# Scale rows and weight units issued earlier, and the slot work of the second-last expert one step sooner, in a one-core retention and expert kernel

## The chip, the cores and the metric

One core of one Trainium2 chip runs the whole kernel. The metric is the device time of one launch in microseconds. The kernel before took 427.85 us (median of three runs, 426.66 to 427.98). All times inside the kernel are counted from the start of the span of one profiled execution.

Engines: TensorE (PE, with its weight loads PEld), VectorE (DVE), ScalarE (ACT), GpSimd (POOL) and SyncE (SP). SP does no arithmetic here: it issues nearly all transfers between DRAM and the on-chip memory, in the order of the program, and where one of them has to wait, all behind it wait too. POOL issues the transfers that pick rows by an index list (gather) or scatter them.

## The reference, cut to what matters

```python
# 1 retention: q, k, v are (4, 8, 768, 64)
for t in range(768):
    state = gamma * state + outer(k[t], v[t]);  y[t] = scale * q[t] @ state
x = y as (3072 tokens, 512)
# 2 each token goes to one of 8 experts
e = argmax(x @ w_gate)
scale = softmax(x @ w_gate)[e] * sigmoid(x @ w_output_gate)[e]
x[token] = scale * (relu(x[token] @ w1[e]) @ w2[e])      # w1 512x1024, w2 1024x512
# 3 soft slots: 32 slots, 4 for each of 8 second experts
logits = x @ phi
slot_input = softmax(logits, over tokens).T @ x
slot_out   = relu(slot_input @ w1b[e]) @ w2b[e]
out = softmax(logits, over slots) @ slot_out
```

## The kernel before, in words

The kernel has three stages. The retention stage walks over 24 tiles of 128 tokens and writes the rows `x` to a DRAM table `xs`. Each row of `xs` has 512 values and behind them the token's scale (tile `sv`), which is written by a transfer of its own, `scale_put`. The last three tiles' scales are computed after the loop over the tiles (`gate_scale`), from line 694 on. There too a table `wps` of partial products is written in two halves of 512 KB, the second (L726) waiting for ACT's last copies into `fsum`.

Then the tokens of one expert at a time are gathered from `xs` (tile `xg`, L755, 3 or 4 gathers of up to 128 rows for each expert), scaled (L902 or L904), transposed (`x_mm`, L911) and multiplied. The first gather needs the index list `xidx` (L746) and every row of `xs`. All engines pass a branch (L868) there, whose body is for experts that are over their capacity.

The expert stage takes the 8 experts in turn, and each expert in 8 steps `f` (the count `g` runs over all 64 steps). In step `g` PE makes a block of the hidden layer (`l1`, L933, 12 products), ACT rectifies it (L938), and the weight block for step `g + 2` is split in two parts, `wh` by ACT (L222) and `wl` by DVE (L223), from a tile `r` that SP has loaded (`load_w`, L214). The products go into one of two buffers in turn, so step `g` needs the rectified block of step `g - 2` to be out. The second layer isn't formed: its product with `phi` is (`wq_mm`, tile `wps`, L243), from units `wt` of 512 KB (`wq_load`, L234), three for each expert, in a pool of three. For the first expert the three units wait until all its gathers have landed; the units of the second expert are issued behind steps 3 and 4, behind the loads of two or more `r` tiles and of a part of the table (`wpp`, L949).

Beside the steps of an expert the slot work of the expert before it is done (`behind`): sums of logits (`lps` L963, `lsum` L984), the exponentials, the product of the hidden blocks with them (`slot_h`, tile `gps`, L1046), copies of that to `gr` (`slot_s`, L1053), their sum (`slot_t`, tile `gsum`, L1059), the product with the second weights `w` (`slot_in`, tile `slo`, L1068; loaded by L954), and the sum into `acc` (`slot_acc`, L1072). For the second-last expert `slot_in` and `slot_acc` come behind the last step of the last expert, among the first operations of the last expert's own slot work, which nothing overlaps.

Each engine runs its instructions in the order in which the program is written; pools of tiles decide when a load may start. In the last expert's steps SP also starts to load the weights `m` of the last stage (`load_m2`, L269, 128 tiles of 256 KB in all) into tiles that come free. The last stage multiplies the slots by these weights (`fh` L1246, `so` L1283), and 24 output transfers of 256 KB each end the kernel.

Of the kernel before, what the change touches and what calls it, by code (L numbers as in the profile page):

```python
# [22 lines left out]
E = 8  # L23
# [4 lines left out]
KD = DM // 128  # L28
KF = FF // 128
# [9 lines left out]
IO, UMM, QA = 6, 2, 1  # L39
# [98 lines left out]
def retention_moe_kernel(ctx, tc, qt, kt, kn, vn, gates, moe_w1, moe_w2,  # L138
                         moe2_phi, moe2_w1, moe2_w2, consts, out, dbg=None):
    nc = tc.nc  # L140
    _, off, ni, na, nb = _consts()
# [60 lines left out]
    def after(inst, earlier):  # L202
        for other in earlier:
            tc.add_manual_dep(inst.ins, other.ins.name,
                              mybir.DependencyInfo(mybir.DependencyClass.Sync, mybir.DependencyReason.DATA),
                              reason="order of transfers")
# [9 lines left out]
    def split_w(g):  # L216
        if g >= G:
            return
        t = raw_t.pop(g)
        hi = whl.tile([128, DM], F32R, tag="wh1", name="wh1")  # L220
        lo = whl.tile([128, DM], F32R, tag="wl1", name="wl1")
        nc.scalar.activation(out=hi, in_=t, func=ACTF.Copy)  # L222
        nc.vector.tensor_tensor(out=lo, in0=t, in1=hi, op=ALU.subtract)  # L223
        w1_t[g] = (hi, lo)
# [7 lines left out]
    def wq_load(k, q, n, pool, tag):  # L232
        t = pool.tile([128, n * FF], F32, tag=tag, name="wt")
        get = nc.sync.dma_start(out=t, in_=moe_w2[1, bass.ds(er[k], 1), :, q * FF:(q + n) * FF].rearrange("o p d -> (o p) d"))  # L234
        for h in range(n):
            wtt[k, q + h] = [t[:, h * FF + g * 256:h * FF + g * 256 + 256] for g in range(4)]
        return get
# [8 lines left out]
    def wq_add(k):  # L246
        nc.vector.tensor_tensor(out=parts[k], in0=wacc.pop(k), in1=parts[k], op=ALU.add)
# [28 lines left out]
    def load_m2(pool, tag, w=1):  # L276
        w = min(w, NM2 - len(m2_t))
        if w > 0:
            m2_into(pool.tile([128, w * 512], F32, tag=tag, name="m2"), w, (pool, tag, w) if w < 3 else None)
# [37 lines left out]
    with ExitStack() as pa:  # L317
# [96 lines left out]
        def first_copy(e):  # L414
            nc.scalar.copy(out=fsum[:, e, :], in_=facc.pop(e))
# [170 lines left out]
        def gate_scale(i):  # L586
            if i not in ENDS:
                return
            t, n = ENDS[i]
            sm = gs.pop(t)  # L590
            one_ = lambda k: sm[:, k, 0, 0:n]
            nc.vector.tensor_reduce(out=one_(8), in_=sm[:, 6, 0:n, :], axis=AX.X, op=ALU.add)
            nc.vector.tensor_scalar(out=one_(9), in0=one_(7), scalar1=1.0, scalar2=None, op0=ALU.add)
            nc.vector.scalar_tensor_tensor(out=one_(10), in0=one_(8), scalar=1e-9, in1=one_(9), op0=ALU.add, op1=ALU.mult)
            scl[t] = sc2.tile([128, 3, DX - DM], F32, tag="sv", name="sv")
            nc.vector.reciprocal(out=scl[t][:, 0:n, :], in_=bc(one_(10), n, DX - DM))
# [39 lines left out]
        def scale_put(i):  # L636

            if i not in ENDS:
                return
            t, n = ENDS[i]  # L640
            nc.sync.dma_start(out=xs[t * 128:(t + n) * 128, DM:DX].rearrange("(u p) o -> p u o", p=128), in_=scl.pop(t)[:, 0:n, :])
# [81 lines left out]
            first_mm(e)  # L723
        for e in range(4, E):
            first_copy(e)
        nc.sync.dma_start(out=wps[:, 4:E], in_=fsum[:, 4:E])  # L726
        gate_scale(i)
        scale_put(i)
        load_er(0)
        load_w(0)  # L730
        load_w(1)
# [158 lines left out]
    with ExitStack() as pb:  # L890
# [60 lines left out]
        def load_w2(e, fs, pool=w2p, tag="w2"):  # L951
            for f in fs:
                w2n[e, f] = pool.tile([128, DM], F32, tag=tag, name="w2")
                nc.sync.dma_start(out=w2n[e, f], in_=moe_w2[0, bass.ds(er[e], 1), :, f * DM:(f + 1) * DM].rearrange("o p d -> (o p) d"))  # L954
# [109 lines left out]
        def slot_in(e):  # L1064
            ps = slo[e] = ps_1.tile([128, DM], F32, tag="C", name="slo")
            for f in range(KF):
                i = f % 4
                nc.tensor.matmul(out=ps[32 * i:32 * i + 32, :], lhsT=gts[e][:, f, :], rhs=w2n.pop((e, f)),  # L1068
                                 start=(f < 4), stop=(f >= 4), skip_group_check=True)

        def slot_acc(e):
            nc.vector.scalar_tensor_tensor(out=acc, in0=acc, scalar=sms.pop(e)[:, 4:5], in1=slo.pop(e), op0=ALU.mult, op1=ALU.add)  # L1072

        def behind(e, f):

            if not 0 <= e < E:
                return
            if f == 0:
                logits(e, 1)
                if e:  # L1080
                    slot_in(e - 1)
                h_tr(e, 6)
                h_tr(e, 7)
            elif f == 1:
                logit_sum(e)
            elif f == 2:
                p_exp(e)
            elif f == 3:
                p_tr(e)
            elif f == 4:  # L1090
                slot_h(e)
                c_tr(e)
            elif f == 5:
                slot_s(e)
                c_exp(e)
            elif f == 6:
                slot_t(e)
                c_put(e)
            if 2 < f < 7:
                load_w2(e, (2 * f - 6, 2 * f - 5))  # L1100

        load_er(1)

        after(wq_load(0, QA, 1, wup, "wu"), gets[0])
        for q in range(QA + 1, KD):
            wq_load(0, q, 1, wup, "wu")
        part_load(0)
# [8 lines left out]
        for g in range(G):  # L1116
            e, f = divmod(g, KF)
            if f == 0:
                load_er(e + 2)
            if e + 1 < E and f < len(XT[e + 1]):  # L1120

                gather(e + 1, (f,))
                if f:
                    after(gets[e + 1][f], [relu[-1]])
            split_w(g + 2)
            if e and f == 1:

                if e > 1:
                    slot_acc(e - 2)
                logit_parts(e - 1)  # L1130
            if g < G - 3:
                load_w(g + 3)
            else:
                load_m2(wraw, "r1")
            if g > 3 and g % 2 and len(m2_t) < NPRE:
                load_m2(m2p, "m2", 2)
            if f in (4, 5) and e + 1 < E:
                for j in range(2 * f - 8, min(2 * f - 6, len(XT[e + 1]))):
                    x_scale(e + 1, j)
            if f == KF - 1 and e + 1 < E:  # L1140

                xps = x_mm(e + 1, "ABDr", sorted(((j, kk) for kk in range(KD) for j in range(len(XT[e + 1]))),
                                                 key=lambda b: XT[e + 1][b[0]] < 128))
                l1(g, lambda: [x_split(e + 1, ps) for ps in xps])
            else:
                l1(g)
            behind(e - 1, f)


            if g == UMM:  # L1150
                wq_mm(0, ps_1, "C")
                wq_add(0)
            if f == (1 if e else UMM):
                wq_turn(e, sp.tile([128, KF, NS], F32, tag="wp", name="wp"))
            if e + 1 < E:
                if f == (2 if e else 3):
                    part_load(e + 1)
                if e == 0 and f in (3, 4):
                    for q in ((1, 2), (3,))[f - 3]:
                        wq_load(1, q, 1, wup, "wu")  # L1160
                if f == (3 if e else 6):

                    wq_mm(e + 1, ps_1, "A" if e else "C")
                    wq_add(e + 1)
            if g == KF - 1:
                wq_load(2, 1, 1, wup, "wu")
                wq_load(2, 2, 1, wup, "wu")
            if g == KF:
                wq_load(2, 3, 1, wup, "wu")
            if e and e + 2 < E and 4 <= f < 7:  # L1170
                wq_load(e + 2, f - 3, 1, wup, "wu")
            elif G - 13 < g < G - 9:
                load_m2(wup, "wu", 2)
            if g == G - 6:
                load_w2(e, range(4), xp, "xy")
            if g >= G - 2:

                for i, tag in enumerate(("wh1", "wl1")):
                    load_w2(e, (2 * f - 8 + i,), whl, tag)
            if f == 4:  # L1180
                logits(e, 0)
            if f == 5:

                mask(e)
            if f >= 5:
                h_tr(e, 2 * f - 10)
                h_tr(e, 2 * f - 9)
        e = E - 1
        logits(e, 1)
        logit_parts(e)  # L1190
        slot_in(e - 1)
        slot_acc(e - 1)
        logit_sum(e)
        load_m2(whl, "wh1")
        load_m2(whl, "wl1")
        for _ in range(KD):
            load_m2(xtp, "xh")
            load_m2(xtp, "xl")
        for _ in range(8):
            load_m2(w2p, "w2")  # L1200
        h_tr(e, 6)
        h_tr(e, 7)
        for _ in range(NH):
# [20 lines left out]
        c_exp(e)  # L1224
        c_put(e)
        for _ in range(4):
            load_m2(xp, "xy")
        for _ in range(2):
            load_m2(whl, "wh1")
            load_m2(whl, "wl1")  # L1230
# [162 lines left out]
```

## Time and profile before

| | |
|---|---|
| median of 3 runs | 427.85 us (426.66 to 427.98) |
| profiled execution | 427.91 us |
| its span, first to last instruction | 426.1 us |
| outside the span | 1.8 us |
| PE / DVE / ACT / POOL busy | 379.5 / 260.9 / 165.6 / 108.0 us |
| moved by DMA | 132.96 MB, 312 GB/s over the span |
| chain that ended last | PE 73%, DVE 9%, DMA 7%, ACT 4% |

The terms of the chain say what was late at each moment. An average over the span says little: PE is busy for 89% of it, but the places where it waits are few and each has its own cause, and behind the expert stage the DMA engines are full while PE isn't.

### The profile page before, as it was taken

The numbers are of one execution on the slowest core, as the hardware profiler recorded it, in microseconds if no ns is written. First come the engines' busy times: TensorE is split into PE (matmuls) and PEld (weight loads), VectorE is DVE, ScalarE is ACT, GpSimd is POOL, SyncE is SP. The second block draws the span as 40 slices with busy tenths as digits, with TensorE's granted clock in tenths as the row PEclk, the third lists the DMA queues.
The fourth block names the chain that finished last, engine by engine and source line by source line (L and its number), as shares of the span: only waits on it lengthen the run. The fifth ranks groups of instructions, "written<-read, shape, count | busy, mean of one in ns | idle before, by whom it ended". The sixth has DMA issues, their size and how long they took to land.

```text
span 426.1 us, 11539 instructions
## 1 busy us (share of the span) xinstructions
PE 379.5 (89%) x4407; PEld 284.7 (67%) x4407; DVE 260.9 (61%) x681; ACT 165.6 (39%) x368; POOL 108.0 (25%) x116
## 2 busy tenths in 40 slices
PE   2989999998639999999999999999999996799990
PEld 2877777786428777777877877787679872225560
DVE  1698989988723276575675664864757655414250
ACT  1532322223324365454545545543555421112232
POOL 2203333321033113043252431620612122020020
PEclk9999999999958999999999999999999999699996
DMA  7999999999958798977969969969778789999998
GB/s 270 403 420 334 307 314 338 304 280 327 251 161 316 222 368 287 385 279 237 403 225 329 376 203 357 358 192 386 248 223 338 238 263 318 388 398 407 392 346 289
DMA packets 68002, 132.96 MB, mean 312 GB/s; under 512 B 10628, under 2 KB 30082, under 8 KB 65634
## 3 DMA queue, kind: packets, MB, share of 16 engines
q1 hardware_dynamic: 61154, 120.17, 80.2%
q0 software_dynamic: 3344, 8.34, 6.5%
q10 hardware_dynamic: 3440, 3.63, 2.6%
q8 instruction: 36, 0.59, 0.6%
q14 instruction: 28, 0.23, 0.2%
HBM read 117.89 MB, written 14.25 MB: 310 GB/s over the span
## 4 chain that ended last, share of the span: by engine, by line
PE 73%; DVE 9%; DMA 7%; ACT 4%; issue 3%; SPq 1%; ACTq 1%; another core or an unknown queue 0%; POOL 0%; POOLq 0%; DVEq 0%
PE hps L933 30%; PE s L447 5%; PE o L480 5%; PE gps L1046 5%; PE fh L1246 4%; PE slo L1068 4%; PE so L1283 3%; PE lps L963 3%; PE wps L243 3%; PE o L471 2%; DMA r<-in_moe_w_dram 2%; DMA raw<-in_qt_dram 2%; PE xps L911 2%; PE st L494 2%; PE g L545 2%
## 5 line engine op out<-in xcount | busy, mean ns | idle before, releaser
L933 PE MATMUL hps<-xh,wh 128*128 128x416 f32 (+2 forms) x256 | 92.9, 363 | 0.1
L933 PE MATMUL hps<-xl,wh 128*128 128x416 f32 (+2 forms) x256 | 90.1, 352 | 0.3 <-DVE xl L921 0.2
L933 PE MATMUL hps<-xh,wl 128*128 128x416 f32 (+2 forms) x256 | 89.5, 350 | 0.0
L223 DVE TENSOR_TENSOR wl<-r,wh 128x512 fp32r<-128x512 f32 x64 | 43.4, 680 | 57.9 <-ACT wh L222 47.3
L938 ACT ACTIVATE h<-hps 128x416 f32<-128x416 f32 (+2 forms) x64 | 32.6, 510 | 68.7 <-PE hps L933 67.1
L222 ACT ACTIVATE wh<-r 128x512 fp32r<-128x512 f32 x64 | 40.2, 630 | 48.9 <-DMA r<-in_moe_w_dram 38.2
L933 PEld LDWEIGHTS hps<-xh,wh 128*128 128x128 f32 x256 | 48.7, 190 | 15.5 <-issue 13.4
L1029 POOL DMA_INDIRECT ctok<-ce,xidx x29 | 30.1, 1040 | 100.9 <-DVE ce L1026 94.5
L933 PEld LDWEIGHTS hps<-xl,wh 128*128 128x128 f32 x256 | 48.8, 190 | 2.2 <-DVE xl L921 1.2
L933 PEld LDWEIGHTS hps<-xh,wl 128*128 128x128 f32 x256 | 48.7, 190 | 0.6
L755 POOL DMA_INDIRECT xg<-xs,xidx x29 | 30.4, 1047 | 70.3 <-ACT h L938 49.5
L457 DVE TENSOR_TENSOR sS<-s,csa 128x512 f32<-128x512 f32 x48 | 30.4, 674 | 14.4 <-PE s L447 14.4
L447 PE MATMUL s<-raw 64*128 64x128 f32 x384 | 31.9, 301 | 8.0 <-DMA raw<-in_qt_dram 7.7
L945 DVE STREAM_TRANSPOSE hB<-h 128x416 f32<-128x416 f32 (+2 forms) x64 | 34.4, 576 | 0.0
L447 PEld LDWEIGHTS s<-raw 64*128 64x128 f32 x384 | 26.7, 201 | 10.7 <-DMA raw<-in_qt_dram 5.5
L480 PE MATMUL o<-sS,raw 128*64 128x128 f32 x384 | 27.1, 285 | 0.0
L512 ACT COPY xT<-o 128x512 f32<-128x512 f32 x24 | 13.9, 580 | 32.0 <-PE o L480 32.0
L429 POOL TENSOR_TENSOR k<-raw,cs 128x512 f32<-128x512 f32 x20 | 21.9, 1110 | 16.4 <-DMA raw<-in_qt_dram 11.1
L911 PE MATMUL xps<-cs,xg 128*128 128x128 f32 (+2 forms) x116 | 15.7, 285 | 9.2 <-ACT wh L222 7.9
L480 PEld LDWEIGHTS o<-sS,raw 128*64 128x64 f32 x384 | 21.2, 140 | 3.7 <-issue 3.4
L1046 PE MATMUL gps<-hB,pd 32*32 32x256 f32 x816 | 19.8, 394 | 3.6 <-DVE pd L1000 3.6
L911 PEld LDWEIGHTS xps<-cs,xg 128*128 128x128 f32 (+2 forms) x116 | 12.8, 148 | 13.6 <-issue 11.7
(178 smaller groups left out, 532.6 us busy)
## 6 DMA issues: line engine op xcount, KB each, us to landing
m<-in_moe_w_dram SPq DMA_DIRECT2D x41, 512.0 KB
wt<-in_moe_w_dram SPq DMA_DIRECT2D x32, 512.0 KB
r<-in_moe_w_dram SPq DMA_DIRECT2D x64, 256.0 KB
w<-in_moe_w_dram SPq DMA_DIRECT2D x64, 256.0 KB
m<-in_moe_w_dram SPq DMA_DIRECT2D x36, 256.0 KB
xs<-xr SPq DMA_DIRECT2D x32, 192.0 KB
raw<-in_kt_dram SPq DMA_DIRECT2D x5, 1024.0 KB
raw<-in_kn_dram SPq DMA_DIRECT2D x5, 1024.0 KB
```

Of the source, the lines that this page charges most:

```text
L222: nc.scalar.activation(out=hi, in_=t, func=ACTF.Copy)
L223: nc.vector.tensor_tensor(out=lo, in0=t, in1=hi, op=ALU.subtract)
L447: nc.tensor.matmul(out=ps[h][:, p, :], lhsT=kq(i, p, 0)[r], rhs=kq(i, p, 1)[r], start=True, stop=True, tile_position=(64 * h, 0), skip_gro ...
L457: nc.vector.tensor_tensor(out=sS[i][:, h], in0=sps.pop((i, h)), in1=con("dm", 128)[:, 4 * h:4 * h + 4, :], op=ALU.mult)
L480: nc.tensor.matmul(out=o_at(i, p, h), lhsT=vals(i, 2 * p + h), rhs=s[:, h, p, :], start=(i % NCH == 0 and n < 4), stop=True, skip_group_ch ...
L755: gets.setdefault(e, []).append(nc.gpsimd.indirect_dma_start(out=t[0:r, :], out_offset=None, in_=xs[:, :], in_offset=bass.IndirectOffsetOn ...
L911: nc.tensor.transpose(out=ps[kk][:, j * 128:j * 128 + r], in_=xg[e][j][0:r, kk * 128:(kk + 1) * 128], identity=ident[0:r, 0:r])
L933: nc.tensor.matmul(out=ps, lhsT=a[:, kk * 128:(kk + 1) * 128], rhs=x[e][kk][:, 0:c], start=(n == 0), stop=(n == 11))
L938: relu.append(nc.scalar.activation(out=hs[g][:, 0:c], in_=ps, func=ACTF.Relu))
L945: nc.vector.transpose(out=hB[e][:, 0:NB[e], f, :], in_=hs[e * KF + f][:, 0:c].rearrange("p (b t) -> p b t", t=32))
L1029: put = nc.gpsimd.indirect_dma_start(out=ctok[:, :], out_offset=bass.IndirectOffsetOnAxis(ap=xidx[0:r, e, j:j + 1], axis=0), in_=cn[0:r, j ...
L1046: nc.tensor.matmul(out=ps[a][32 * j:32 * j + 32, :], lhsT=pd[q, b, :], rhs=hB[e][q, b].rearrange("p f t -> p (f t)"), start=(i == 0), stop ...
```

## The change

Five places change. (1) After the loop over tiles, the last scales are put (`scale_put`) ahead of the second half of `wps` on SP. (2) The first unit of the first expert waits for its first two gathers and not for all three. (3) The units of the second expert are issued right behind the products with the first expert's units (`g == UMM`), ahead of what SP issued there before. (4) For the second-last expert, `slot_s` moves from step 5 to 4, `slot_t` from 6 to 5, `slot_in` into step 6 and `slot_acc` into step 7. Its second weights are loaded in steps 1 to 4 and not 3 to 6. (5) In the last expert's first two steps, four `m` tiles are loaded into the buffers of gathered rows, where the last expert's first four weight tiles went; these go to the pool `w2p`, behind `slot_in`, followed by four `m` tiles.

```diff
         for e in range(4, E):
             first_copy(e)
+        gate_scale(i)
+
+        scale_put(i)
         nc.sync.dma_start(out=wps[:, 4:E], in_=fsum[:, 4:E])
-        gate_scale(i)
-        scale_put(i)
         load_er(0)
...
-        def behind(e, f):
+        def behind_one(e, f):
...
-            if 2 < f < 7:
+
+        def behind(e, f):
+            behind_one(e, f)
+            if e >= 0 and 2 < f < 7:
                 load_w2(e, (2 * f - 6, 2 * f - 5))
 
+        def behind_last(e, f):
+
+            if f < 4:
+                behind_one(e, f)
+            elif f == 4:
+                slot_h(e)
+                c_tr(e)
+                slot_s(e)
+            elif f == 5:
+                slot_t(e)
+                c_exp(e)
+            elif f == 6:
+                slot_in(e)
+                c_put(e)
+            elif f == 7:
+                slot_acc(e)
+            if 0 < f < 5:
+                load_w2(e, (2 * f - 2, 2 * f - 1))
+            elif f == 6:
+                load_w2(e + 1, range(4))
+                for _ in range(4):
+                    load_m2(w2p, "w2")
+
         load_er(1)
 
-        after(wq_load(0, QA, 1, wup, "wu"), gets[0])
+        after(wq_load(0, QA, 1, wup, "wu"), gets[0][:2])
...
             split_w(g + 2)
+            if G - KF <= g < G - KF + 2:
+                load_m2(xp, "xy")
+                load_m2(xp, "xy")
...
-            behind(e - 1, f)
+            (behind if e < E - 1 else behind_last)(e - 1, f)
...
             if g == UMM:
                 wq_mm(0, ps_1, "C")
                 wq_add(0)
+                for q in range(QA, KD):
+                    wq_load(1, q, 1, wup, "wu")
...
-                if e == 0 and f in (3, 4):
-                    for q in ((1, 2), (3,))[f - 3]:
-                        wq_load(1, q, 1, wup, "wu")
...
-            if g == G - 6:
-                load_w2(e, range(4), xp, "xy")
...
-        slot_in(e - 1)
-        slot_acc(e - 1)
...
-        for _ in range(8):
-            load_m2(w2p, "w2")
...
         for _ in range(4):
-            load_m2(xp, "xy")
+            load_m2(w2p, "w2")
```

SP's order behind the loop over tiles: `xs<-xr` are the rows of the last tiles, `xs<-sv` their scales, `wps<-fsum` the halves of the table.

```order
 L721 DMA wps<-fsum 128x1024
-L726 DMA wps<-fsum 128x1024
 L641 DMA xs<-sv 128x3x16
+L729 DMA wps<-fsum 128x1024
 L198 TENSOR_LOAD ordi
```

The scales now stand between the two halves of the table.

SP's order in the first expert's steps before, from the load of step 6's weights (`r`) on; `ISA` rows set registers:

```order
L214 ISA
L214 DMA r_3706<-in_moe_w_dram 128x512
L949 ISA
L949 DMA wpp<-wps 128x256
L234 ISA
L234 DMA wt<-in_moe_w_dram 128x1024
L234 ISA
L234 DMA wt<-in_moe_w_dram 128x1024
L214 ISA
L214 DMA r_3733<-in_moe_w_dram 128x512
L234 ISA
L234 DMA wt<-in_moe_w_dram 128x1024
```

And in the changed kernel, the same six transfers:

```order
L234 ISA
L234 DMA wt<-in_moe_w_dram 128x1024
L234 ISA
L234 DMA wt<-in_moe_w_dram 128x1024
L234 ISA
L234 DMA wt<-in_moe_w_dram 128x1024
L214 ISA
L214 DMA r_3712<-in_moe_w_dram 128x512
L950 ISA
L950 DMA wpp<-wps 128x256
L214 ISA
L214 DMA r_3735<-in_moe_w_dram 128x512
```

The three units have gone ahead of the weights of steps 6 and 7 and of the part of the table.

PE's order behind the last expert's last step before (`hps` is the hidden block, `slo` the second-last expert's product with the second weights):

```order
L933 MATMUL hps<-xh,wl_6594 128x384
L963 MATMUL lps<-h,wp 32x384 x4
L1068 MATMUL slo<-w_6503,gt 32x512
L1068 MATMUL slo<-w_6505,gt 32x512
L1068 MATMUL slo<-w_6584,gt 32x512
L1068 MATMUL slo<-w_6586,gt 32x512
L1068 MATMUL slo<-w_6624,gt 32x512
L1068 MATMUL slo<-w_6626,gt 32x512
L1068 MATMUL slo<-w_6670,gt 32x512
L1068 MATMUL slo<-w_6672,gt 32x512
L984 MATMUL lsum<-ls,same_r 128x384
L984 MATMUL lsum<-ll,same_r 128x384
```

And the same place in the changed kernel:

```order
L934 MATMUL hps<-xh,wl_6607 128x384
L964 MATMUL lps<-h,wp 32x384 x4
L985 MATMUL lsum<-ls,same_r 128x384
L985 MATMUL lsum<-ll,same_r 128x384
L1047 MATMUL gps<-hB,pd 32x256 x48
```

The eight products have left the place between `lps` and `lsum`; they stand one hidden block earlier.

## Rows read from the trace of the kernel before

**Rows 1.** The waits behind line 755, 113 to 117.4 us: duration min/median/max

```profile
L755 POOLq EVENT_SEMAPHORE  x4: 43/43/2550, 113.4 to 114.3; - x4
```

**Rows 2.** SP's issues in order of time, 110 to 132 us: start, us, engine, line

```profile
112.94 0.36 SPq L726 DMA_DIRECT2D wps<-fsum  x1
113.39 0.39 SPq L641 DMA_DIRECT2D xs<-sv  x1
...
125.83 1.42 SPq L234 DMA_DIRECT2D wt<-in_moe_w_dram  x3
```

**Rows 3.** DVE in order of time, 112 to 126 us; in brackets the idle time before

```profile
112.45 0.45 DVE L596 RECIPROCAL sv<-sm 128x48 f32<-128x48 f32 x1
...
115.25 0.19 DVE L746 TENSOR_REDUCE xidx<-lx 128x4 int32<-128x32 f32 x1
...
125.64 0.48 DVE L902 TENSOR_SCALAR xg<-xg 128x512 f32<-128x512 f32 x1 [2.02 <-DMA xg<-xs,xidx]
```

**Rows 4.** Chain that ended last, 104 to 165 us: start, us, what

```profile
120.60 5.02 DMA xg<-xs,xidx
...
127.37 8.80 PE hps L933 x36
...
144.32 5.31 DMA wt<-in_moe_w_dram
```

**Rows 5.** ACT in order of time, 122 to 151 us

```profile
123.06 0.72 ACT L904 ACTIVATE xg<-xg 128x512 f32<-128x512 f32 x1 [0.16 <-DMA xg<-xs,xidx]
...
134.47 0.63 ACT L222 ACTIVATE wh<-r 128x512 fp32r<-128x512 f32 x1 [2.09 <-DMA r<-in_moe_w_dram]
...
140.85 1.32 ACT L904 ACTIVATE xg<-xg 128x512 f32<-128x512 f32 x2
142.08 0.48 ACT L938 ACTIVATE h<-hps 128x384 f32<-128x384 f32 x1
147.94 0.63 ACT L222 ACTIVATE wh<-r 128x512 fp32r<-128x512 f32 x1 [5.38 <-DMA r<-in_moe_w_dram]
```

**Rows 6.** PE in order of time, 106 to 170 us

```profile
136.10 1.50 PE L243 MATMUL wps<-wt,phi 128*32 128x256 f32 x24
...
144.92 0.33 PE L933 MATMUL hps<-xh,wh 128*128 128x384 f32 x1
...
149.68 0.64 PE L243 MATMUL wps<-wt,phi 128*32 128x256 f32 x8 [1.52 <-DMA wt<-in_moe_w_dram]
```

**Rows 7.** Stretches: length, busy us of PE, PEld, DVE, ACT, POOL; clock, DMA share, GB/s

```profile
118.30:131.80 13.50, 7.58 (x25) 6.27 (x26) 4.82 (x9) 4.02 (x8) 3.71 (x4) 0.50 0.66 204
...
344.00:350.00 6.00, 6.00 (x45) 4.71 (x42) 2.31 (x7) 1.73 (x5) 0.00 (x0) 1.00 0.79 267
350.00:357.00 7.00, 5.79 (x38) 3.21 (x37) 4.77 (x12) 0.98 (x2) 2.98 (x3) 1.00 0.86 280
370.00:410.00 40.00, 38.95 (x449) 18.27 (x449) 12.76 (x48) 9.34 (x22) 4.45 (x5) 0.96 1.04 395
```

**Rows 8.** PE in order of time, 352 to 370 us

```profile
353.04 0.49 PE L963 MATMUL lps<-h,wp 128*32 128x384 f32 x1
353.23 2.02 PE L1068 MATMUL slo<-w,gt 128*32 128x512 f32 x13
...
355.46 0.33 PE L984 MATMUL lsum<-ll,same_r 128*128 128x384 f32 x1
```

**Rows 9.** DVE in order of time, 326 to 372 us

```profile
354.09 0.56 DVE L971 TENSOR_TENSOR ll<-lps,ls 128x384 fp32r<-128x384 f32 x1 [0.99 <-issue]
355.78 0.75 DVE L1072 SCALAR_TENSOR_TENSOR acc<-acc,smb,slo 128x512 f32<-128x512 f32 x1 [1.14 <-PE lsum L984]
356.45 0.55 DVE L986 TENSOR_TENSOR msk<-lsum,msk 128x384 f32<-128x384 f32 x1
```

**Rows 10.** Chain that ended last, 165 to 350 us: the product `slo` inside a step

```profile
331.37 1.72 PE slo L1068 x16
```

**Rows 11.** SP's issues in order of time, 338 to 358 us

```profile
342.63 5.71 SPq L954 DMA_DIRECT2D w<-in_moe_w_dram  x4
```

More of the change, by code (lines that the diff above doesn't have):

```diff
@@ L725, in retention_moe_kernel @@
             first_copy(e)
-        nc.sync.dma_start(out=wps[:, 4:E], in_=fsum[:, 4:E])
         gate_scale(i)
         scale_put(i)
+        nc.sync.dma_start(out=wps[:, 4:E], in_=fsum[:, 4:E])
         load_er(0)
```

## The prediction

> **What bounds the kernel now.** I read the stretches first, then PE in order of time for the places where it waits, then the chain, and last the engine or queue that each wait names. PE is the bound inside the expert stage: in 344 to 350 us it is busy for all of the 6.00 us [rows 7]. Behind it the transfers are full: from 370 to 410 us the DMA share is 1.04 at 395 GB/s [rows 7]. So a microsecond is won where PE waits, or where bytes of the last stage move earlier. The change touches three such places.
>
> The first is the pause between retention and experts. POOL's first gather stands in a wait that begins at 114.3 and takes 2.55 us, to 116.85 [rows 1]. The list `xidx` is there from 115.25 + 0.19 = 115.44 [rows 3]. What is left to wait for are the writes into `xs`, of which the scales are the last: issued at 113.39, behind the second half of `wps` at 112.94 [rows 2]. The third gather takes 5.02 us [rows 4], DVE scales its tile at 125.64 [rows 3], and the first expert product starts at 127.37 [rows 4].
>
> The second is a wait of PE of 1.52 us at 149.68 for a unit of the second expert [rows 6], which the chain shows as 5.31 us of transfer from 144.32 [rows 4]. The third is the passage behind the last step: `lps` ends at 353.53, and DVE reaches `msk` at 356.45 [rows 8, 9].
>
> **Part 1, the scales and the first units.** The scales are ready at 112.45 + 0.45 = 112.90 [rows 3] and can now be issued some 0.45 us earlier, and their bytes no longer follow 512 KB. At 395 GB/s those are 1.33 us, together 1.78; but the list isn't there before 115.44, so at most 116.85 - 115.44 = 1.41 us can be won, and nothing at least. The first half of `wps` and the rows are still ahead of them, so I take 0.9, two thirds of the upper end. `wps` is later by the scales' own issue of 0.39 us [rows 2]; it is read only after 125.83 [rows 2], which hides that.
>
> Releasing the first unit after two gathers lets three units, 1.5 MB, start beside the third. The second gather's tile is worked on from 123.06 [rows 5], so at 122.2 in the changed kernel; the third would end at 125.64 - 0.9 = 124.7 without them. Between lie 2.5 us in which they meet. The cost is between zero and 2.5 (its rest takes twice as long); the nearest row is the third gather itself, 5.02 us with nothing beside it for most of its time, so it isn't short of bandwidth, and I take 0.2. That leaves 0.7. PE's clock is 0.50 from 118.3 to 131.8 [rows 7], the 1.2 GHz level, after PE had stood idle; 4.4 us of the first expert's products run in it. If the rise follows the work, all 0.7 arrive; if it stays where it is, half. I take **0.6 us won**.
>
> The Trainium skill speaks against this edit. On the page "DMA: Bandwidth & Descriptors", in the section on queues, rings and completion order, it says that each DMA engine takes turns between the queues that have work for it, a packet at a time. The gathers and the units are on different queues, so by that rule the third gather would get every second turn. No row here has both at once.
>
> **Part 2, the units of the second expert.** The wait of 1.52 us goes. In its place: the three units start as their tiles come free, from a third of the 1.50 us product on, 136.10 + 0.50 = 136.6 [rows 6]. Behind them in SP's order, and behind their 1.5 MB, is now the `r` of step 6. ACT splits that tile (0.63), scales two gathered tiles (1.32) and only then rectifies step 4 (0.48), as it did at 140.85 to 142.56 [rows 5]; step 6 takes that buffer and started at 144.92 [rows 6]. The nearest row for an `r` behind three units: issue of the first unit at 125.83 [rows 2], split of the `r` at 134.47 on its landing [rows 5], 8.6 us. By bytes alone, 1.8 MB at 395 GB/s, it is 4.6. With 8.6 step 6 could start at 136.6 + 8.6 + 2.43 = 147.6, 2.7 us late, a net loss of 1.2; with 4.6 nothing is late, a net gain of 1.5. The row had a part of the table and a POOL gather between, so I take 7.0: 146.0, 1.1 us late, **0.4 us won**. ACT's other wait there, 5.38 us for the next `r` at 147.94 [rows 5], loses its cause too, as that `r` no longer stands behind the units; left alone, it would have held the scaled tiles until 147.94 + 0.63 + 1.32 = 149.9, so the unit wait alone was never worth its full 1.52.
>
> **Part 3, the slot work of the second-last expert.** No instruction is added. The product `slo` costs 1.72 us inside a step [rows 10]; in front of `lsum` it took until 353.23 + 2.02 = 355.25 [rows 8]. There it covered the making of `ls` and `ll`, which ends at 354.65 [rows 9]. PE has no idle time in the step that takes it, so `lps` ends 1.72 later, at 355.25. From there 354.65 - 353.53 = 1.12 to `ll`, 0.33 of `lsum`, 0.10 to `msk`: 356.80, against 356.45. `acc`, which stood ahead of `msk` on DVE from 355.78 [rows 9], is out of the way; that is in this sum. So **0.35 us lost**. The ends: 1.37 won if the step hides all of `slo`, 1.72 lost if nothing comes back. `slot_s` and `slot_t` only change steps; ACT's two copies now stand ahead of a weight split, which has a step and a half in hand.
>
> **Part 4, SP's queue at the end.** In step 6 SP meets four weight tiles that may not start before `slo` has read theirs, at about 350. The loads of before at 342.63 to 348.34 and behind them [rows 11] have to wait behind that. From 344 to 350 the kernel before moved 6 x 267 = 1.6 MB [rows 7]; the changed one moves little. Four tiles, 1.05 MB, have gone earlier instead, leaving 0.55 MB. From 350 to 357 the share was 0.86 at 280 GB/s [rows 7]; with a full queue at 395, 0.8 MB more go there. I take **0**, between 0.6 won and 2.7 lost (the 1.05 MB at 395 GB/s, if nothing is made up).
>
> **Sum.** 0.6 + 0.4 - 0.35 = 0.65 us won: 427.91 - 0.65 = 427.26 for the profiled execution. That execution is 0.06 above the median of the runs, so 427.2.
>
> **Rivals.** A: faster. The `r` of step 6 comes in time, and part 1 wins 0.9: 0.9 + 1.5 - 0.35 = 2.05, 425.8. If PE, busy earlier, also leaves the lower clock earlier, up to half of the 4.4 us come on top, 423.6. For it: the DMA engines are not full there, and the split tiles are needed late. Against: the 8.6 us of the row.
>
> B: slower. The hole in SP's queue isn't made up, and the last stage, at a share of 1.04 for 40 us [rows 7], ends later by the 2.7 us: 429.9. It decides from a lag of 1.9 us on (the 0.65 and 1.28). For it: the share, and that everything on SP stands behind one wait. Against: before, 350 to 357 wasn't full, and nothing in the last stage waits for a transfer on PE.
>
> C: change (1) doesn't do what it says, because the gather waits for another transfer or the landing isn't earlier. Then 0.6 are missing: 427.8.
>
> D: the third gather shares its engines with the units and takes all of the 2.5 us longer: 427.2 + 2.3 = 429.5. That is what the turns of the Trainium skill's page would make of it.
>
> **How the numbers follow.** The forecast has 0.46, A 0.33, B 0.10, C 0.06, D 0.05. About 0.3%, 1.28 us, is what a measurement of this kernel can tell from no change: below 426.6 is faster, above 429.1 slower. Faster: A and 0.04 of the forecast's lower edge, 0.37. Slower: B and D, 0.15. Within: 0.48. The forecast's own range is 426.4 to 428.4; the range reaches to A without an early clock and to most of B, 425.0 to 429.3.
>
> **What would show it.** Right: POOL's first wait ends near 116; PE has no wait ahead of its unit products in the first expert, but one of about a microsecond ahead of step 6, with ACT late; `msk` starts 0.3 us later from the end of step 7 of the last expert; SP issues nothing for some 7 us ahead of the second-last expert's `slo`, and the DMA share of the 7 us behind is near 1. Wrong: step 6 not late (A); the third gather's landing not earlier (C, D); output transfers that end later by more than the expert stage does (B).

## The result, and the profile after

| | before | after |
|---|---|---|
| median of 19 runs each | 427.51 us (424.19 to 432.11) | 432.2 us (427.54 to 436.2) |
| ratio | | 1.0089, 95% interval 1.0065 to 1.0113 |
| profiled execution | 427.91 us | 429.17 us |
| its span | 426.1 us | 427.4 us |
| clock over the span | 0.963 | 0.958 |

The change costs 0.89%, 3.8 us. The ratio leaves out the slow runs, among them two of the 19 of the changed kernel, and so is smaller than the quotient of the two medians. The forecast was 427.2 with a range up to 429.3; by the ratio the time is 431.3, outside the range, on the slower side. The profiled execution is one of the shorter ones of the changed kernel and shows only 1.3 us of the loss; the rest is read from the experiments. I take the four parts in turn.

**Part 1: the pause between retention and experts.** POOL in order of time, then SP's issues (start, us, engine, line; the idle time before in brackets), in the changed kernel:

```profile
116.07 1.27 POOL L756 DMA_INDIRECT xg<-xs,xidx  x1 [10.27 <-DVE lim L767]
117.64 1.04 POOL L756 DMA_INDIRECT xg<-xs,xidx  x1 [0.30 <-issue]
118.98 1.01 POOL L756 DMA_INDIRECT xg<-xs,xidx  x1 [0.31 <-issue]
```

```profile
112.61 0.38 SPq L641 DMA_DIRECT2D xs<-sv  x1
113.08 0.44 SPq L729 DMA_DIRECT2D wps<-fsum  x1
...
122.91 1.64 SPq L234 DMA_DIRECT2D wt<-in_moe_w_dram  x3
```

The first gather starts at 116.07, as soon as DVE's short operations behind the list end; and the third at 118.98, where it was 120.60 [rows 4]. The product with the first expert's units starts at 133.75 instead of 136.10 [rows 6], 2.35 us earlier. The first unit is issued only at 122.91, and the third gather's tile is scaled at 123.97, so the two met for some 1.1 us and not for the 2.5 that the prediction reckoned with.

**Part 2: steps 4 to 6 of the first expert.** SP, ACT, PE and the chain in order of time (the chain: start, us, what), and three stretches (length, busy us of PE, PEld, DVE, ACT, POOL, then clock, DMA share, GB/s):

```profile
134.45 1.52 SPq L234 DMA_DIRECT2D wt<-in_moe_w_dram  x3
136.60 0.33 SPq L214 DMA_DIRECT2D r<-in_moe_w_dram  x1
```

```profile
137.60 0.49 ACT L939 ACTIVATE h<-hps 128x384 f32<-128x384 f32 x1 [2.73 <-PE hps L934]
143.45 0.63 ACT L222 ACTIVATE wh<-r 128x512 fp32r<-128x512 f32 x1 [5.37 <-DMA r<-in_moe_w_dram]
143.99 1.32 ACT L905 ACTIVATE xg<-xg 128x512 f32<-128x512 f32 x2
145.21 0.47 ACT L939 ACTIVATE h<-hps 128x384 f32<-128x384 f32 x1
```

```profile
133.75 1.50 PE L243 MATMUL wps<-wt,phi 128*32 128x256 f32 x24
...
145.73 0.53 PE L934 MATMUL hps<-xh,wh 128*128 128x384 f32 x1 [3.00 <-ACT h L939]
146.06 0.52 PE L934 MATMUL hps<-xl,wh 128*128 128x384 f32 x1
...
149.57 1.50 PE L243 MATMUL wps<-wt,phi 128*32 128x256 f32 x24
```

```profile
136.60 6.77 DMA r<-in_moe_w_dram
...
145.73 3.91 PE hps L934 x12
```

```profile
134.40:143.40 9.00, 8.34 (x60) 6.62 (x52) 1.44 (x3) 0.96 (x2) 2.55 (x2) 1.00 0.95 299
143.00:145.70 2.70, 0.00 (x0) 0.00 (x0) 0.69 (x1) 2.25 (x5) 0.00 (x0) 1.00 0.86 333
145.70:149.50 3.80, 3.77 (x12) 3.54 (x12) 2.33 (x4) 2.62 (x5) 0.00 (x0) 0.55 0.67 205
```

The weights `r` of step 6 are issued behind the three units and land 6.77 us later. ACT stands in their split for 5.37 us (0.63 us of work), scales two gathered tiles, and only at 145.21 rectifies step 4. PE, which takes that buffer in step 6, waits 3.00 us. Then there is a second price: after the wait the granted clock is 0.55, the 1.2 GHz level for most of the stretch; the products follow each other at 0.32 us, and the twelve of step 6 take 3.91 us. Twelve take 2.31 at 2.4 GHz (tail, below), so 1.6 us more are lost. The wait of 1.52 us for a unit [rows 6] is gone: the unit product at 149.57 has none. Net, by the end of that product: 3.0 + 1.6 - 1.52 = 3.1 us lost where the forecast had 0.4 won.

A part of it comes back. Before, PE then waited for DVE ahead of the second expert's `lsum`, and from its last product of one hidden block (160.03) to the first of the next (161.53) it took 1.50 us; the changed kernel has no wait there and takes 0.55 (160.79 to 161.34). The first two rows are of before, the third of the changed kernel; L243 is here the third expert's unit product:

```profile
161.24 0.45 PE L984 MATMUL lsum<-ll,same_r 128*128 128x384 f32 x1 [0.37 <-DVE ll L971]
...
166.48 1.50 PE L243 MATMUL wps<-wt,phi 128*32 128x256 f32 x24
```

```profile
166.29 1.50 PE L243 MATMUL wps<-wt,phi 128*32 128x256 f32 x24
```

From the first expert's unit product to the third's it takes 30.38 us before and 32.54 in the changed kernel: 2.2 us lost. With part 1's gain the changed kernel is 0.19 us ahead at the third product, so in this pair of executions the front loses nothing, and what its span is longer, 1.3 us, is lost behind it. Over all traces that distance is 32.5 to 35.3 us in the five kernels with three units ahead of step 6's weights, and 29.4 to 32.1 in the nine others; the means, 33.7 and 30.8, lie 2.9 us apart.

**Part 3: the passage behind the last step.** The chain, and DVE, in the changed kernel:

```profile
347.88 2.31 PE hps L934 x12
350.19 1.85 PE slo L1069 x16
352.04 2.29 PE hps L934 x12
354.33 1.43 PE lps L964 x8
...
355.78 0.50 ACT ls L971
...
356.30 0.57 DVE ll L972
...
356.92 0.46 PE lsum L985
```

```profile
352.19 0.75 DVE L1073 SCALAR_TENSOR_TENSOR acc<-acc,smb,slo 128x512 f32<-128x512 f32 x1 [0.49 <-PE slo L1069]
...
357.46 0.56 DVE L987 TENSOR_TENSOR msk<-lsum,msk 128x384 f32<-128x384 f32 x1 [0.61 <-PE lsum L985]
```

`slo` costs its full time in the step, and `ls`, `ll` and `lsum` now stand bare behind `lps`. `msk` starts 10.11 us after ACT began to rectify step 5 of the last expert (347.35); before it was 9.26 (356.45 [rows 9] - 347.19). The two rows of ACT, before and in the changed kernel:

```profile
347.19 0.49 ACT L938 ACTIVATE h<-hps 128x384 f32<-128x384 f32 x1 [4.13 <-PE hps L933]
```

```profile
347.35 0.49 ACT L939 ACTIVATE h<-hps 128x384 f32<-128x384 f32 x1 [1.92 <-PE hps L934]
```

**Part 4: SP's queue.** SP's last issue ahead of the pause, and the first behind it; the stretches of [rows 7]:

```profile
340.58 1.64 SPq L269 DMA_DIRECT2D m<-in_moe_w_dram  x2
351.20 2.11 SPq L955 DMA_DIRECT2D w<-in_moe_w_dram  x4
```

```profile
344.00:350.00 6.00, 6.00 (x55) 4.43 (x40) 3.47 (x9) 1.98 (x5) 0.00 (x0) 1.00 0.08 27
350.00:357.00 7.00, 6.27 (x40) 3.02 (x38) 3.85 (x10) 1.47 (x3) 2.98 (x3) 1.00 0.55 170
370.00:410.00 40.00, 38.67 (x442) 18.31 (x444) 13.70 (x51) 9.10 (x21) 4.28 (x5) 0.96 1.04 397
```

The hole is there: nothing is issued for 9 us, and 344 to 357 us moves 6 x 27 + 7 x 170 = 1,350 KB where before it was 6 x 267 + 7 x 280 = 3,560 KB (GB/s times us gives KB). That looks like the cause of the loss. The experiments say that it isn't. Nor do the traces show it to cost PE anything: behind 364 us its products wait only for DVE and ACT, before and after, and never longer than 1.5 us, and its weight loads wait for a transfer for 0.7 us at most.

### The profile page after: what moved, and what is told of

Read it like the earlier page. It is cut to its first block, busy times and chain, and to the rows that moved or that the text cites. A ratio compares the mean times of both kernels' runs of the same rounds, so it can differ in the third digit from the quotient of the medians.

```text
span 427.4 us, 11538 instructions
## 1 busy us (share of the span) xinstructions
PE 380.6 (89%) x4407; PEld 285.9 (67%) x4407; DVE 260.9 (61%) x681; ACT 164.6 (39%) x368; POOL 108.1 (25%) x116
## 4 chain that ended last, share of the span: by engine, by line
PE 40%; DMA 21%; DVE 4%; ACT 4%; issue 1%; ACTq 1%; SPq 0%; DVEq 0%
PE hps L934 24%; DMA r<-in_moe_w_dram 12%; DMA m<-in_moe_w_dram 4%; PE slo L1069 4%; PE fh L1269 3%; DMA w<-in_moe_w_dram 3%; PE lps L964 2%; PE gps L1047 2%; PE xps L912 2%; PE wps L243 2%; DMA two<-in_moe_w_dram 2%; DVE wl L223 1%; ACT wh L222 1%; ACT ot L1366 1%; DMA out_dram<-ot 1%
## 5 line engine op out<-in xcount | busy, mean ns | idle before, releaser
L447 PEld LDWEIGHTS s<-raw 64*128 64x128 f32 x384 | 26.9, 203 | 10.4 <-DMA raw<-in_qt_dram 5.6
L429 POOL TENSOR_TENSOR k<-raw,cs 128x512 f32<-128x512 f32 x20 | 22.3, 1135 | 15.7 <-DMA raw<-in_qt_dram 13.3
```

The source lines that it names most:

```text
L447: nc.tensor.matmul(out=ps[h][:, p, :], lhsT=kq(i, p, 0)[r], rhs=kq(i, p, 1)[r], start=True, stop=True, tile_position=(64 * h, 0), skip_gro ...
```

## The experiments

Each kernel was timed in five rounds beside the kernel before; the brackets hold the 95% interval of the ratio, and 1% is 4.3 us. Three theories stood at the start: HOLE (part 4), PASSAGE (part 3), FRONT (part 2).

**1. The front alone** (changes 1, 2, 3). The last expert and the last stage are as before.

> The kernel before with changes (1), (2) and (3) alone; the slot work and the tiles at the end stay as before. Theory HOLE (the loss sits in SP's queue at the end, where transfers stand behind the second-last expert's product): this kernel is level with before, -0.5 to +0.5 us, since in the changed kernel the steps of the last expert start 0.15 us later than before and nothing of the loss is there yet. Theory PASSAGE (the loss is PE's later passage behind the last step): the same, -0.5 to +0.5. Theory FRONT (the units put ahead of the weights of step 6 cost more in most executions than in the one profiled): +1.5 to +3.5 us.

Measured: 1.0043 (1.0019 to 1.0068), +1.8 us. Part of the loss is in the front, so neither HOLE nor PASSAGE can be the whole of it. In its trace PE waits 4.02 us ahead of step 6, and the granted clock behind it is 0.50 to 0.57 until 152 us, so that the second expert's unit product takes 1.91 us as well, for 1.50.

**2. The tail alone** (changes 4, 5).

> The kernel before with changes (4) and (5) alone. HOLE: +3 to +4.5 us, all of the loss. PASSAGE: +1 us, what the profile shows for the later start of the maximum behind the last step. FRONT: +0.5 to +1.3 us.

Measured: 1.0098 (1.0061 to 1.0136), +4.2 us, from six runs between 427.45 and 433.56. The profiled one is the shortest of them; it has `msk` at 10.12 and the hole, and nothing that is worth 4 us. The size is the one that HOLE gave, and above that of PASSAGE and FRONT. But numbers 1 and 2 together are 6.0 us where the whole change costs 3.8, and the same tail costs 1.4 on another front (number 8 against 10).

**3. The change without its tiles** (change 5 undone), so that no load stands behind `slo`:

```diff
-            elif f == 6:
-                load_w2(e + 1, range(4))
-                for _ in range(4):
-                    load_m2(w2p, "w2")
...
+            if g == G - 6:
+                load_w2(e, range(4), xp, "xy")
```

> The changed kernel with (5) undone: the slot work is one step sooner, but the last expert's first four weight tiles go where they went before and wait for no product, so SP's queue has no new wait. HOLE: the loss shrinks to PE's 0.9 us: +0.5 to +1.5 against before, and the DMA bytes from 344 to 357 us are near the 3.5 MB of before and not 1.35. PASSAGE: the loss stays whole, +3 to +4.5. FRONT: as the front alone, plus 0.9.

Measured: 1.0100 (1.0057 to 1.0143), +4.3 us: no better than the change. Its stretches, where SP's queue isn't held:

```profile
345.20:351.20 6.00, 6.00 (x58) 4.40 (x40) 4.83 (x13) 2.98 (x7) 0.00 (x0) 1.00 0.91 315
351.20:358.20 7.00, 6.42 (x40) 3.06 (x38) 3.99 (x11) 1.47 (x3) 2.98 (x3) 1.00 0.56 191
```

The first six microseconds move 315 GB/s instead of 27, and the time stays. So HOLE isn't the cause, against what number 2 alone suggests.

**4. The waiting loads later** (the tiles behind the other loads of the last two steps).

> The changed kernel with the waiting loads moved: the last expert's first four weight tiles and the four m tiles behind them are issued after the two pairs of loads for other buffers that stood behind them on SP, so fewer transfers stand behind the product. HOLE: part of the loss comes back, +1 to +2.5 us against before, since SP's pause still is there for the tiles themselves but ends with other loads already under way. PASSAGE and FRONT: no difference from the changed kernel, +3 to +4.5.

Measured: 1.0109 (1.0070 to 1.0148), +4.7 us: nothing came back.

**5. The scales and the first units alone** (changes 1, 2).

> The kernel before with changes (1) and (2) alone. Theory GATHER GAIN (the earlier scales let POOL's first gather start about 1.3 us earlier, 1.6 to 1.8 us behind the last product of the index list where it was 3.0, and no transfer pays for it): -1.0 to -1.5 us against before. Theory LOST IN THE QUEUE (the units that start beside the third gather, or a later wait for a weight load, take it back): -0.3 to +0.5.

Measured: 0.9978 (0.9938 to 1.0017), -0.9 us. The interval touches both theories. In the trace POOL starts its first gather 2.1 us behind the start of the index product (3.0 before), and step 6's weights, issued ahead of all three units, make nobody wait: ACT splits them directly behind step 3, and rectifies step 4 at 138.41.

```profile
136.27 0.49 ACT L939 ACTIVATE h<-hps 128x384 f32<-128x384 f32 x1 [2.04 <-PE hps L934]
136.66 0.62 ACT L222 ACTIVATE wh<-r 128x512 fp32r<-128x512 f32 x1
137.18 1.32 ACT L905 ACTIVATE xg<-xg 128x512 f32<-128x512 f32 x2
138.41 0.48 ACT L939 ACTIVATE h<-hps 128x384 f32<-128x384 f32 x1
```

**6. The units of the second expert alone** (change 3):

```diff
                 wq_add(0)
+                for q in range(QA, KD):
+                    wq_load(1, q, 1, wup, "wu")
...
-                if e == 0 and f in (3, 4):
-                    for q in ((1, 2), (3,))[f - 3]:
-                        wq_load(1, q, 1, wup, "wu")
```

> The kernel before with change (3) alone. Theory LATE WEIGHTS (the weights of step 6 land behind the three units, ACT stands in their split for them and rectifies step 4 only behind it, PE waits 3 to 5 us ahead of step 6): +2 to +3.5 us against before, and the wait of PE ahead of step 6 is in the trace. Theory UNITS FREE (the product with the units gains what step 6 loses): -0.5 to +0.5.

Measured: 1.0101 (1.0065 to 1.0137), +4.3 us: somewhat above the range that LATE WEIGHTS gave, and UNITS FREE falls. ACT and PE show the same two prices as the changed kernel:

```profile
145.82 0.63 ACT L222 ACTIVATE wh<-r 128x512 fp32r<-128x512 f32 x1 [6.09 <-DMA r<-in_moe_w_dram]
```

```profile
148.10 0.69 PE L933 MATMUL hps<-xh,wh 128*128 128x384 f32 x1 [3.72 <-ACT h L938]
148.59 0.53 PE L933 MATMUL hps<-xl,wh 128*128 128x384 f32 x1
```

**7. The slot work alone** (change 4).

> The kernel before with change (4) alone, tiles and loads of m as before. Theory PASSAGE (the product slo no longer covers the way from lps to lsum): +1.0 to +1.5 us, and from the rectifying of step 4 of the last expert to the maximum's first operation 15.2 us in place of 14.4. Theory HOLE (the loss of the tail came with the tiles): 0 to +0.5.

Measured: 1.0033 (0.9992 to 1.0074), +1.4 us, and `msk` at 10.12. The size is PASSAGE's, but the interval takes in HOLE's 0 to 0.5. Counted from step 4, as the expectation did, the way is 13.3 us and not 15.2: in this trace ACT waits 2.96 us for a weight tile and rectifies step 4 at 345.25, 3.99 us behind step 3 where it was 2.09, while step 5 isn't later for it. Counted from step 5 the shift is 1.36 (see below).

**8. The whole change, with the units one step later**, so that only step 6's weights go ahead of them:

```diff
-            if g == UMM:
...
+            if g == UMM + 1:
                 for q in range(QA, KD):
                     wq_load(1, q, 1, wup, "wu")
```

> The changed kernel with the units of the second expert issued one step later, behind the load of step 6's weights and still ahead of the part of the table and of step 7's weights. LATE WEIGHTS: PE's wait ahead of step 6 goes; +0.5 to +2 us against before, 2 to 3.5 less than the changed kernel, unless ACT now stands for step 7's weights. UNITS FREE: no difference from the changed kernel, +3 to +4.5.

Measured: 1.0005 (0.9967 to 1.0043), +0.2 us. One load moved past three gives 0.84%, 3.6 us, back, slightly more than LATE WEIGHTS gave; UNITS FREE falls. ACT splits step 6's weights without a wait and PE doesn't wait:

```profile
139.06 0.62 ACT L222 ACTIVATE wh<-r 128x512 fp32r<-128x512 f32 x1
139.58 1.33 ACT L905 ACTIVATE xg<-xg 128x512 f32<-128x512 f32 x2
140.81 0.48 ACT L939 ACTIVATE h<-hps 128x384 f32<-128x384 f32 x1
```

```profile
134.83 1.50 PE L243 MATMUL wps<-wt,phi 128*32 128x256 f32 x24
...
145.83 1.50 PE L243 MATMUL wps<-wt,phi 128*32 128x256 f32 x24
```

From the first expert's unit product to the second's it takes 11.0 us here, and 15.8 in the changed kernel.

**9. The scales alone** (change 1).

> The kernel before with change (1) alone. Theory SCALES (all of the gain of (1) and (2) is the earlier issue of POOL's first gather): -0.8 to -1.3 us against before, as (1) and (2) together, with the first gather 1.6 to 1.8 us behind the index product where it was 3.0. Theory UNITS (the earlier units carry a part): -0.3 to -0.6 only.

Measured: 0.9982 (0.9945 to 1.0020), -0.8 us, with the gather 1.8 us behind the index product. It is level with (1) and (2) together, so SCALES is the better reading, but the interval reaches no change.

**10. The front with the units one step later**, tail as before.

> The kernel before with (1) and (2), and the three units of the second expert behind the load of step 6's weights but ahead of the part of the table and of step 7's weights; the tail as before. Theory ADDITIVE (the units in that place cost and give nothing, and the moved slot work costs 1.4 us): -0.8 to -1.5 us against before, level with (1) and (2) alone. Theory UNITS EARLIER HELP (the wait of 1.5 us ahead of the units' product was a real loss): -1.8 to -2.8.

Measured: 0.9971 (0.9941 to 1.0000), -1.2 us: ADDITIVE. Of all kernels this one has the lowest ratio; it isn't told apart from number 5 or 9.

**11. As number 8, without the tiles.**

> As the kernel with the units one step later and the whole tail of the change, but without change (5), so no load on SP stands behind the second-last expert's product. Theory HOLE SMALL: 0.3 to 1.0 us less than that kernel with the tiles (which took +0.2 us against before), so -0.8 to 0 against before. Theory HOLE NOTHING: the same time, -0.2 to +0.6.

Measured: 1.0017 (0.9988 to 1.0046), +0.7 us, against +0.2 with the tiles and the hole: HOLE NOTHING is the better reading. The two intervals are too wide to exclude HOLE SMALL.

**12. One unit ahead of step 6's weights**, not three.

> The kernel before with one of the second expert's three units ahead of step 6's weights in place of three; the other two one by one in the next two steps. Theory BYTES (the weights land later by the time of the bytes ahead of them, some 1.5 us for 0.5 MB, and they had some 1 us in hand): PE waits 0 to 1 us ahead of step 6, -0.5 to +0.8 us against before. Theory ORDER (any unit ahead holds the weights back, as SP or the queue must get through it first): PE waits 3 us or more there as with three units, +2.5 to +4.5.

Measured: 0.9985 (0.9948 to 1.0022), -0.6 us: BYTES. (Its profiled execution took 429.0 us where the median is 427.0, so only this place is read from it.) ACT waits a little, PE not at all:

```profile
143.37 0.63 ACT L222 ACTIVATE wh<-r 128x512 fp32r<-128x512 f32 x1 [1.76 <-DMA r<-in_moe_w_dram]
```

From the start of the unit product (137.28) to that split it takes 6.1 us with one unit ahead; with three it is 9.7 in the changed kernel and 10.4 in number 6. So each further unit of 512 KB costs some 2 us ((9.7 - 6.1) / 2 and (10.4 - 6.1) / 2), and the first of them fits into what the weights had in hand.

## Why the prediction was wrong, step by step

**Part 2 is the step that failed**: "I take 7.0: 146.0, 1.1 us late, 0.4 us won". It measured 3.1 us lost at the second expert's unit product, 2.2 of them still there at the third's. The mechanism was named, with the same engine, instruction and step; three sizes were off.
- The time from the first unit's issue to the weights' landing. I went down from the row's 8.6 us [rows 2, 5] to 7.0, toward a sum by bytes. It was 143.37 - 134.45 = 8.9 in the changed kernel and 145.8 - 136.1 = 9.7 in number 6. The rate of 395 GB/s didn't hold: the stretch moved 299 GB/s, 2.7 MB in 9 us, of which the units and the weights are 1.8. The rest is of gathers, further weights and a part of the table.
- The clock. Lateness was priced as lateness, with nothing for the clock. The step behind the wait ran at 1.2 GHz, 1.6 us more. So it was behind all five waits of 3.0 to 4.7 us ahead of step 6 (granted clock 0.50 to 0.59 at first); behind the wait of 1.52 us before it was 1.00 (149.5 to 152 us).
- The unit wait of 1.52 us. I used it as a fixed gain. With the units where they were before, the traces have between nothing (number 2) and 0.52 + 1.27 us (number 9). And number 10, where the wait is gone, isn't told apart from number 5, where it is 1.11 us.

Measured as differences, change (3) costs 4.3 us against the units where they were (number 6), and 3.1 (number 1 against 10) and 3.6 (the change against number 8) against the units one step later. Rival A, step 6's weights in time, falls with this.

**Part 3 had the mechanism and too small a size**: 0.35 lost, measured 1.36. `msk` begins 8.76 us (to 0.01) after the rectifying of step 5 in all six experiments with the tail as before, and 10.12 in five of six with the slot work moved (10.31 in number 3) and in the changed kernel. Half a microsecond of the miss is the row that I took as "before": there DVE's `acc` didn't start until 355.78 although `slo` ended at 355.25, and `msk` came at 9.26. The rest is `slo` at 1.85 for 1.72, 0.2 us more in the turns between it and the steps, and 1.72 from `lps` to `msk` where I had 1.55. In time it is +1.4 us (number 7, whose interval reaches no change) or +2.0 (number 11 against 10). Number 2 measured more, 2.6 to 5.8 us, and what its longer runs spend there I have not seen in a trace. The record has one hint: its two runs with a mean clock of 0.962 took 427.45 and 429.50 us, the four with 0.952 to 0.958 took 429.84 to 433.56. What lowered the clock isn't known. That stays open.

**Part 1 held.** Across the traces the first gather starts 1.6 to 2.1 us behind the index product with change (1) and 3.0 without, 0.9 to 1.4 us won for the 0.9 that I took. In time it is -0.9 (number 5), -0.8 (number 9) and -1.2 (number 10); the first two intervals reach past no change. Rival D, the third gather slowed by the units, falls: from its issue to its tile's scaling it takes 4.99 us in the changed kernel (118.98 to 123.97), and 4.3 to 5.5 in all kernels with change (2), against 4.8 to 5.6 in those without. So the turns of the page "DMA: Bandwidth & Descriptors" of the Trainium skill cost nothing that is seen here; but gather and units lay side by side for at most 1.1 to 1.7 us in these traces (from the first unit's issue to the scaling), so a longer meeting is not tested. Rival C falls with the same rows.

**Part 4 held in its price, not in its reason, which makes it luck.** The loads weren't made up in the 7 us behind the pause (share 0.55, not near 1). With the hole or without it the kernels are level (numbers 8 and 11, the change and number 3: the hole's is the shorter time by 0.5 us in both pairs). That speaks against the 2.7 us of B; a cost below 1 us would not show. So B, the rival on the right side, was on it for a reason that the runs speak against. Why a hole of a good megabyte costs nothing isn't shown row by row. That PE's products wait for no transfer behind 364 us, before or after, fits transfers of `m` that had as much in hand.

**The sum.** By the runs' times -0.9 (part 1, number 5), +3.1 to +4.3 (part 2), +1.4 (part 3, number 7) and 0 (part 4) make 3.6 to 4.8 us slower, for 3.8 measured. The profiled pair, for which the forecast was 427.26, adds up otherwise: -0.2 us at the third expert's unit product, 0.35 lost from there to step 5 of the last expert, 0.85 in part 3 and 0.3 behind `msk` make its 1.3. Had part 2 been priced by the row alone and not moved toward the bytes, the forecast would have been 427.2 + 0.4 + 1.2 = 428.8; the clock's 1.6 makes 430.4.

## What to carry to other kernels

Where a load is put ahead of another on one queue, look for who stands in line behind the one that is passed: here ACT's short split held the rectifying that PE needed. Price its delay by a row in which the same kind of load stood behind such bytes, not by bytes over the best rate, and allow for a lower clock behind the wait: it fell behind all five of 3.0 to 4.7 us here. And before using a short wait of one profiled execution as a gain, ask how the same place could fall in another.

## What was not expected of the hardware

The same chain of operations, from `msk` to the first `mps` product behind the last expert, took 10.5 us in number 9 and 13.8 in number 10, with the same instructions. The difference is the granted clock. PE in number 9, where it fell only at the end (0.97 from 356.6 to 366.0), and in number 10 (0.63 from 356.1 to 369.0):

```profile
356.69 2.12 PE L1047 MATMUL gps<-hB,pd 32*32 32x256 f32 x96 [3.14 <-DVE pd L1001]
...
360.81 1.92 PE L1069 MATMUL slo<-w,gt 128*32 128x512 f32 x16 [0.57 <-DVE gt L1063]
```

```profile
356.19 3.45 PE L1047 MATMUL gps<-hB,pd 32*32 32x256 f32 x96 [3.15 <-DVE pd L1001]
...
362.09 3.41 PE L1069 MATMUL slo<-w,gt 128*32 128x512 f32 x16 [0.57 <-DVE gt L1063]
```

PE had stood idle equally long before (3.14 and 3.15 us), so the wait alone doesn't decide whether the clock falls at once. Such differences may be a part of the spread of one kernel's runs (423.3 to 429.2 for number 9): the four runs of number 9 with a mean clock of 0.966 or more took 423.3 to 424.7, the others 424.9 to 429.2. They aren't all of it: eight runs of number 10 had 0.963 or 0.964 and took 424.8 to 428.1.
